# A two-layer attention and MLP block, forward and backward, in one kernel: weights read in fewer passes, half of one product on VectorE, PSUM rearranged for it

## The chip, the cores and the metric

The kernel runs on one core of a Trainium2 chip. The metric is the device time of one execution, in microseconds (us), smaller being better. The kernel before the change takes 559.78 us (median of three runs, 557.5 to 561.76). Each execution is classed as fast or slow by its time against the fastest run of the same kernel. The span in a profile is 1.5 us shorter than the time of the same execution (560.3 beside 561.76 for the kernel before).

In the text, PE is TensorE (matmuls), DVE is VectorE, ACT is ScalarE, POOL is GpSimd and SP is SyncE. PE, DVE and ACT do arithmetic here; SP issues loads and the writes of zeros, POOL issues the stores of results.

## The reference, cut to what matters

There is one token, D = 1024, 32 query heads in 4 groups, a window of the last 4096 of 32768 cached keys, F = 3584, all in bf16. The same two layers are applied twice with the same weights, and the kernel returns the output and the gradients of eight inputs.

```python
def _fwd_reference(A_x, A_k_cache, A_v_cache, A_wq, A_wo, B_x, B_w1, B_b1, B_w2):
    # _A_ref: attention over the window, q = x @ wq, result @ wo
    def _B_ref(x, w1, b1, w2):
        h = x @ w1 + b1
        act = h * tanh(softplus(h))                 # Mish
        return act @ w2
    x = A_x
    x = x + _A_ref(_layernorm(x), A_k_cache, A_v_cache, A_wq, A_wo)   # layer 1, "A1"
    x = x + _B_ref(_layernorm(x), B_w1, B_b1, B_w2)                   # layer 2, "B2"
    x = x + _A_ref(_layernorm(x), ...)                                # layer 3, "A3"
    x = x + _B_ref(_layernorm(x), ...)                                # layer 4, "B4"
    return x

_out, _vjp = jax.vjp(_f, A_x, A_k_cache, A_v_cache, A_wq, A_wo, B_w1, B_b1, B_w2)
return (_out, *_vjp(grad_out))
```

(The lines are shortened.) Three consequences matter. All products have one column, so a weight that passes through PE is used once per pass: forward as it lies, backward after a transpose on PE (eight 128x128 transposes into PSUM, then a copy back by ACT or DVE). The gradients of w1, w2, wq, wo, and of K and V inside the window, are sums of two outer products, which must be written out in full: 78 parts of 448 or 512 KB. And the gradients of the caches outside the window are zeros, 112 writes of 512 KB that depend on nothing and can be placed anywhere.

## The kernel before: the parts that matter

Everything runs in program order on each engine. The PSUM pools of the first part add up to 16 KB per partition: four transpose tiles of 2 KB ("pt"), one of 4 KB ("pbig"), two accumulators of 2 KB ("pacc").

```python
pt = tc.alloc_tile_pool(name="pt", bufs=4, space=PSUM)       # 4 x 2 KB
pbig = tc.alloc_tile_pool(name="pbig", bufs=1, space=PSUM)   # 4 KB
pacc = tc.alloc_tile_pool(name="pacc", bufs=1, space=PSUM)   # acc and sm, 2 KB each
...
def zeros(n):                                    # n zero writes on the SP queue
    for _ in range(min(n, len(zero_jobs))):
        nc.sync.dma_start(zero_jobs.pop(0), zt[:])

def xpose2(halves):                              # 2 x 8 transposes, then two copies
    pss = []
    for blocks, dst in halves:
        ps = psum1([P, 8, P], BF16, "tps")
        for b, ap in enumerate(blocks):
            nc.tensor.transpose(ps[:, b, :], ap, ident_bf[:])
        pss.append(ps)
    for (blocks, dst), ps in zip(halves, pss):
        evac(dst, ps...)                         # DVE or ACT, whichever has less to do
...
# order of the work: w1 is read 4 times, w2 3 times
x1, sA1 = attn_fwd(x0, "A1", True)
x2, sB2 = mlp_fwd(x1, "B2", None)        # w1, w2
x3, sA3 = attn_fwd(x2, "A3", False)
x4, sB4 = mlp_fwd(x3, "B4", gcolb)       # w1, then w2 forward and w2 * grad_out
g3, g3b = mlp_bwd_w1(gcol, "B4", sB4, "A3")   # w1
g2, g2b = attn_bwd(g3, g3b, "A3", sA3, True, "B2")
mlp_bwd_w2(g2b, "B2", sB2)               # w2
g1, g1b = mlp_bwd_w1(g2, "B2", sB2, "A1")     # w1
g0, g0b = attn_bwd(g1, g1b, "A1", sA1, False, "X0")
zeros(1000)                              # all zero writes not yet issued
```

When the last gradient of x is there, the three PSUM pools are released and replaced by four output tiles of 4 KB. An output part is made by four matmuls into two tiles, a cast of each tile to bf16 (one on DVE, one on ACT, as a rule), and one store on the POOL queue:

```python
pacc.release(); pbig.release(); pt.release()
pools["p2"] = tc.tile_pool(name="p2", bufs=4, space=PSUM)    # 4 x 4 KB
...
for c in range(nblk // 2):
    st = stage_tile([P, 2, D], "st_t")
    pss = [psum2([P, 1024], FP32, "ops") for _ in range(2)]
    for i in range(2):
        for tt in range(2):
            b = 2 * c + tt
            outer(R, b % 4, (b // 4) * P, i * 512, pss[tt][:, i * 512:(i + 1) * 512])
    for tt in range(2):
        ev_out(st[:, tt, :], pss[tt][:])         # cast PSUM -> SBUF
    nc.gpsimd.dma_start(out_v[c], st[:])
```

Of the kernel before, what the change touches and what calls it, by code (L numbers as in the profile page):

```python
# [14 lines left out]
P = 128  # L15
# [3 lines left out]
NB = 5  # L19
NR = 8  # L20
# [3 lines left out]
def kernel(  # L24
# [47 lines left out]
    pt = tc.alloc_tile_pool(name="pt", bufs=4, space=bass.MemoryType.PSUM)  # L72
    pbig = tc.alloc_tile_pool(name="pbig", bufs=1, space=bass.MemoryType.PSUM)
    pacc = tc.alloc_tile_pool(name="pacc", bufs=1, space=bass.MemoryType.PSUM)
# [21 lines left out]
    rows0 = work.tile([P, 512], BF16, name="rows0", tag="e32", padded_shape=[P, 2 * WC])  # L96
# [36 lines left out]
    def evac(out_ap, in_ap, cd, ca):  # L133
        if ev[0] + cd <= ev[1] + ca:
            ev[0] += cd
            nc.vector.tensor_copy(out_ap, in_ap)  # L136
        else:
            ev[1] += ca
            nc.scalar.copy(out_ap, in_ap)  # L139
# [12 lines left out]
    def psum1(shape, dtype, name):  # L152
        if "p2" in pools:
            return psum2(shape, dtype, name)
        return shaped(pt.tile([P, 512 if dtype == FP32 else 1024], dtype, name=name, tag="pt"), shape)

    def psum2(shape, dtype, name):
        if "p2" in pools:
            return shaped(pools["p2"].tile([P, 1024 if dtype == FP32 else 2048], dtype, name=name, tag="p2"), shape)
        return shaped(pbig.tile([P, 1024 if dtype == FP32 else 2048], dtype, name=name, tag="big"), shape)  # L160

    def xpose2(halves):

        pss = []
        for blocks, dst in halves:
            ps = psum1([P, 8, P], BF16, "tps")
            for b, ap in enumerate(blocks):
                nc.tensor.transpose(ps[:, b, :], ap, ident_bf[:])  # L168
            pss.append(ps)
        for (blocks, dst), ps in zip(halves, pss):  # L170
            n = len(blocks)
            evac(dst, ps[:, 0:n, :].rearrange("p b c -> p (b c)"), 0.08 * n + 0.03, 0.11 * n + 0.15)
# [18 lines left out]
    xq = []  # L191

    def fill(n):
        for _ in range(min(n, len(xq))):
            xpose2([nat_blocks(ap) for ap in xq.pop(0)])
# [98 lines left out]
    def row_layout(col32, name):  # L294
        x = work.tile([P, G, DH], BF16, name=name, tag="rx", bufs=2)
        ps = psum1([P, P], BF16, "rps")
        nc.tensor.transpose(ps[:, 0:P], col32[:], ident_bf[:])
        for g in range(G):
            nc.vector.tensor_scalar(out=x[:, g, :], in0=ps[:, 0:P], scalar1=gmask[:, g:g + 1], scalar2=None, op0=ALU.mult)  # L299
        return x  # L300
# [29 lines left out]
    def to_kpart(src, name):  # L330
        ps = psum1([P, TJ, P], BF16, "kps")
        for j in range(TJ):
            nc.tensor.transpose(ps[:, j, :], src[:, j * P:(j + 1) * P], ident_bf[:])
        dst = work.tile([P, TJ, P], BF16, name="kpart", tag="e32", padded_shape=[P, 2 * TJ, P])
        h = TJ // 2
        nc.vector.tensor_copy(dst[:, 0:h, :], ps[:, 0:h, :])
        nc.scalar.copy(dst[:, h:, :], ps[:, h:TJ, :])
        return dst

    def attn_fwd(x_col, lname, first):  # L340
        n32, n_bf, rstd = ln_fwd(x_col, lname)
        sv = dict(n32=n32, rstd=rstd)
        pad = pad_tile("q_pad")
        acc = acc_tile(HQ)
        wo_ld = {}
        if first:
            for t in range(TD):
# [4 lines left out]
            load_kv(keep, K_t, k_v, "K")  # L352
            load_kv(vpool, V_t, v_v, "V")
            for c in range(NR):
                wo_load(c)
        for t in range(TD):
            for h in range(HQ):
                mm(acc[:, h:h + 1], wq_t[2 * t + h // 16][:, (h % 16) * P:(h % 16 + 1) * P], n_bf[:, t:t + 1],
                   t == 0 and h == 0, t == TD - 1)
        sv["qrep"] = pad_cols(pad, acc[:], scale, f"q_{lname}")  # L360
        if first:
            for g in range(G):
                for u in range(2):
                    xpose2([nat_blocks(flat(K_t[g])[:, (2 * u + k) * 1024:(2 * u + k + 1) * 1024]) for k in range(2)])
        else:
            for w in wq_t:
                xq.append([w[:, k * 1024:(k + 1) * 1024] for k in range(2)])
        big = psum2([P, WC], FP32, "big")
        rows_mm(big, pad, K_t)
        if not first:  # L370
            for g in range(G):
                for u in range(2):
                    xq.append([flat(K_t[g])[:, (2 * u + k) * 1024:(2 * u + k + 1) * 1024] for k in range(2)])
# [4 lines left out]
        m32 = work.tile([1, NC, 32], FP32, name="m32")  # L378
# [5 lines left out]
        e32 = work.tile([P, WC], FP32, name="e32", tag="e32")  # L384
        ssum = work.tile([P, 1], FP32, name="ssum")
        nc.scalar.activation(e32[:], big[:], ACT.Exp, bias=nm[:, 0:1], scale=1.0, accum_out=ssum[:, 0:1])
# [5 lines left out]
        nc.vector.tensor_scalar(out=p_bf[:], in0=e32[:], scalar1=rs[:, 0:1], scalar2=None, op0=ALU.mult)  # L392
# [4 lines left out]
        if not first:  # L397
            for g in range(G):
                for u in range(2):
                    xq.append([flat(V_t[g])[:, (2 * u + k) * 1024:(2 * u + k + 1) * 1024] for k in range(2)])  # L400
# [5 lines left out]
        o_row = work.tile([HQ, P], BF16, name="o_row")  # L406
# [9 lines left out]
        for i, c in enumerate(order):  # L416
            w = wo_kept[c] if c < NR else wo_load(c)
            if i == NB - 1:
                zeros(Z["A1" if first else "A3"])
            fwd_rows2(yacc, w, c, o_bf, i == 0, i == NO - 1)  # L420
        x_new = keep.tile([P, TD], FP32, name=f"x_{lname}")
        nc.vector.tensor_add(x_new[:], x_col[:], yacc[:])
        return x_new, sv

    def mlp_fwd(x_col, lname, g_bf):
# [4 lines left out]
        for i in range(2 * TD):  # L430
            t, hf = i // 2, i % 2
            w = w1_load(i)
            if i == NB - 1:
                zeros(Z[lname])
# [4 lines left out]
            if g_bf is not None:  # L439
                zeros(1 if i >= 2 else 0)  # L440
                fill(2)
        h = work.tile([P, TF], FP32, name="h")
        nc.vector.tensor_add(h[:], hacc[:], b1_f[:])
        hm = work.tile([P, TF], FP32, name="hm")
        nc.vector.tensor_scalar(out=hm[:], in0=h[:], scalar1=20.0, scalar2=None, op0=ALU.min)
        u = work.tile([P, TF], FP32, name="u")
        nc.scalar.activation(u[:], hm[:], ACT.Exp)
        w_ = work.tile([P, TF], FP32, name="w_")
        nc.vector.scalar_tensor_tensor(out=w_[:], in0=u[:], scalar=2.0, in1=u[:], op0=ALU.add, op1=ALU.mult)
        r = work.tile([P, TF], FP32, name="r")  # L450
        nc.vector.tensor_scalar(out=r[:], in0=w_[:], scalar1=2.0, scalar2=None, op0=ALU.add)
        nc.vector.reciprocal(r[:], r[:])
        t_f = work.tile([P, TF], FP32, name="t_f")
        nc.vector.tensor_mul(t_f[:], w_[:], r[:])
        a_bf = pair_col("a", lname, TF)
        nc.vector.tensor_mul(a_bf, h[:], t_f[:])

        v1 = work.tile([P, TF], FP32, name="v1")
        nc.vector.scalar_tensor_tensor(out=v1[:], in0=t_f[:], scalar=1.0, in1=r[:], op0=ALU.add, op1=ALU.mult)
        v2 = work.tile([P, TF], FP32, name="v2")  # L460
        nc.vector.tensor_scalar(out=v2[:], in0=u[:], scalar1=1.0, scalar2=None, op0=ALU.add)
        nc.vector.reciprocal(v2[:], v2[:])
        nc.vector.tensor_mul(v2[:], v2[:], u[:])
        nc.vector.tensor_mul(v1[:], v1[:], v2[:])
        nc.vector.tensor_mul(v1[:], v1[:], h[:])
        dact = keep.tile([P, TF], FP32, name=f"dact_{lname}")
        nc.vector.scalar_tensor_tensor(out=dact[:], in0=v1[:], scalar=2.0, in1=t_f[:], op0=ALU.mult, op1=ALU.add)
        sv["dact"] = dact
        acc = acc_tile(TD + TF)
        yacc, dacc = acc[:, 0:TD], acc[:, TD:]  # L470
        held = []
        for c in range(NW2):
            w = w2_load(c)
            fwd_rows2(yacc, w, c, a_bf, c == 0, c == NW2 - 1)
            if g_bf is not None:
                if c >= 2:
                    zeros(c % 2)
                xpose_rows2(w)
                if held:
                    bwd_rows2(dacc, held.pop(), c - 1, g_bf)  # L480
                held.append(w)
        if g_bf is not None:
            bwd_rows2(dacc, held.pop(), NW2 - 1, g_bf)
            dh_of(dacc, lname, sv)
        x_new = keep.tile([P, TD], FP32, name=f"x_{lname}")
        nc.vector.tensor_add(x_new[:], x_col[:], yacc)
        return x_new, sv

    def dh_of(dacc, lname, sv):
        dh = keep.tile([P, TF], FP32, name=f"dh_{lname}")  # L490
        nc.vector.tensor_mul(dh[:], dacc, sv["dact"][:])
# [3 lines left out]

    def mlp_bwd_w2(g_bf, lname, sv):
        dacc = acc_tile(TF)
        ws = {}

        def T(c):  # L500
            ws[c] = w2_load(c)
            if c == NB - 1:
                zeros(Z["bw2"])
            xpose_rows2(ws[c])

        pipe(list(range(NW2)), T, lambda c, i: bwd_rows2(dacc, ws.pop(c), c, g_bf, started=i > 0))
        dh_of(dacc[:], lname, sv)

    def mlp_bwd_w1(g_col, lname, sv, nxt):
# [3 lines left out]
        def T(i):  # L513
            w = w1_load(i)
            ws[i] = w
            zeros(1 if i % 8 == 7 else 0)
# [11 lines left out]
    def attn_bwd(g_col, g_bf, lname, sv, first, nxt):  # L528
        dacc = acc_tile(HQ)
        pad = pad_tile("do_pad")  # L530
        ws = {}
        loaded = {}

        def T(c):
            if c + NR < NO:
# [283 lines left out]
```

## Time and profile before

| stage of the kernel before | ends at, us | length, us |
|---|---|---|
| layer 1 forward | 78.4 | 78.4 |
| layer 2 forward | 117.5 | 39.1 |
| layer 3 forward | 158.6 | 41.1 |
| layer 4 forward and its input gradient | 265.2 | 106.6 |
| layer 3 backward | 319.8 | 54.6 |
| layer 2: w2 backward | 344.0 | 24.2 |
| layer 2: w1 backward | 374.6 | 30.6 |
| layer 1 backward | 426.9 | 52.3 |
| outputs | 560.3 | 133.4 |

The stage ends were read from the timeline. Three lines of the page of the profile of the kernel before give the span, the clock of PE over 40 slices of it (in tenths of full speed, so a 5 is half) and the bytes:

```profile
span 560.3 us, 15939 instructions
...
PEclk9996555555569996677976599767755555555555
...
HBM read 89.14 MB, written 98.58 MB: 335 GB/s over the span
```

The windows view gives, for a stretch from A to B (us), its length, each engine's busy time, then the granted PE clock, the busy share of the 16 DMA engines and the rate. These are stretches of the kernel before: layer 2 forward, layer 4, w2 backward, and the outputs.

```profile
core 0: us, PE busy (x) PEld busy (x) DVE busy (x) ACT busy (x) POOL busy (x), PEclk, DMA share, GB/s
...
78.40:117.50 39.10, 16.53 (x450) 14.43 (x450) 4.00 (x22) 0.72 (x3) 0.00 (x0) 0.50 0.94 359
...
158.60:265.20 106.60, 91.38 (x1870) 89.98 (x1871) 54.55 (x105) 48.70 (x53) 0.00 (x0) 0.82 0.90 324
...
319.80:344.00 24.20, 20.27 (x450) 19.49 (x448) 12.00 (x20) 11.01 (x11) 0.00 (x0) 0.96 0.80 264
...
426.90:560.30 133.40, 93.74 (x559) 36.22 (x559) 93.04 (x118) 86.48 (x86) 45.65 (x80) 0.50 0.83 313
```

The limits change. Layer 2 forward waits for DMA (share 0.94; PE is busy 16.5 of 39.1 us). In layer 4 PE is busy 91.4 of 106.6 us. In the outputs no single busy time fills the stretch; the timeline of the kernel before (start, length, engine, line, operation, count merged into one line, and in brackets the idle time before it and what ended it) shows the reason:

```profile
431.07 4.72 DVE L136 CAST st_t<-ops 128x1024 bf16<-128x1024 f32 x4
...
434.03 0.53 POOL L644 DMA_DIRECT2D out_dram<-st_t  x1 [0.63 <-ACT st_t L139]
...
434.17 3.06 ACT L139 CAST st_t<-ops 128x1024 bf16<-128x1024 f32 x3 [0.18 <-PE ops L188]
...
435.16 0.53 POOL L644 DMA_DIRECT2D out_dram<-st_t  x1 [0.60 <-DVE st_t L136]
...
436.35 0.53 POOL L644 DMA_DIRECT2D out_dram<-st_t  x1 [0.65 <-ACT st_t L139]
```

Four DVE casts follow each other without a gap (4.72 us, 1.18 us each), and the stores leave about 1.16 us apart. While the steady stores run, the casts are the limit. The first store is at 431.7 us.

### The profile page before, as it was taken

The numbers are of one execution on the slowest core, as the hardware profiler recorded it, in microseconds if no ns is written. First come the engines' busy times: TensorE is split into PE (matmuls) and PEld (weight loads), VectorE is DVE, ScalarE is ACT, GpSimd is POOL, SyncE is SP. The second block draws the span as 40 slices with busy tenths as digits, with TensorE's granted clock in tenths as the row PEclk, the third lists the DMA queues.
The fourth block names the chain that finished last, engine by engine and source line by source line (L and its number), as shares of the span: only waits on it lengthen the run. The fifth ranks groups of instructions, "written<-read, shape, count | busy, mean of one in ns | idle before, by whom it ended". The sixth has DMA issues, their size and how long they took to land. (4 is left out here: it accounts for less than half of the span.)

```text
span 560.3 us, 15939 instructions
## 1 busy us (share of the span) xinstructions
PE 384.5 (69%) x7058; PEld 305.6 (55%) x7058; DVE 228.9 (41%) x411; ACT 192.4 (34%) x211; POOL 51.0 (9%) x95
## 2 busy tenths in 40 slices
PE   3384254364589979877966688768675756888790
PEld 3373153362589979867954677768362112146510
DVE  2052000102037753334632155324304866977691
ACT  1041000001027733333530144323102786855591
POOL 2000000000000000000000000000001423433341
PEclk9996555555569996677976599767755555555555
DMA  8999989999799979789599888896998978797986
GB/s 306 416 418 408 414 301 381 400 400 416 265 384 388 409 243 321 259 282 322 205 363 405 351 277 295 273 349 216 418 414 361 383 308 323 305 341 255 301 349 251
DMA packets 51041, 188.76 MB, mean 337 GB/s; under 512 B 5888, under 2 KB 5916, under 8 KB 49948
## 3 DMA queue, kind: packets, MB, share of 16 engines
q1 hardware_dynamic: 40624, 147.87, 69.9%
q0 software_dynamic: 10304, 39.86, 19.0%
q8 instruction: 55, 0.90, 0.6%
q14 instruction: 14, 0.11, 0.1%
q10 hardware_dynamic: 44, 0.01, 0.0%
HBM read 89.14 MB, written 98.58 MB: 335 GB/s over the span
## 5 line engine op out<-in xcount | busy, mean ns | idle before, releaser
L168 PE MATMUL tps<-ident_bf,w_c 128*128 128x128 bf16 x896 | 72.9, 246 | 16.3 <-DMA w_c<-in_B_w_dram 16.0
L188 PEld LDWEIGHTS <-w_c 128*128 128x128 bf16 x1792 | 57.8, 100 | 33.8 <-DMA w_c<-in_B_w_dram 23.8
L139 ACT COPY w_c<-tps 128x1024 bf16<-128x1024 bf16 (+1 forms) x50 | 46.2, 927 | 84.4 <-PE tps L168 79.5
L168 PEld LDWEIGHTS <-w_c 128*128 128x128 bf16 x896 | 62.8, 112 | 17.9 <-DMA w_c<-in_B_w_dram 17.9
L136 DVE COPY w_c<-tps 128x1024 bf16<-128x1024 bf16 (+1 forms) x70 | 46.0, 667 | 64.6 <-PE tps L168 60.8
L139 ACT CAST st_t<-ops 128x1024 bf16<-128x1024 f32 x32 | 31.3, 1014 | 23.4 <-PE ops L188 21.6
L136 DVE CAST st_t<-ops 128x1024 bf16<-128x1024 f32 x28 | 33.0, 1220 | 6.9 <-issue 3.3
L188 PEld LDWEIGHTS <-wo_c 128*128 128x128 bf16 x512 | 16.4, 102 | 22.6 <-DMA wo_c<-in_A_wo_dram 21.8
L188 PE MATMUL acc<-a_pair,w_c 128*128 128x1 bf16 x448 | 15.8, 165 | 17.2 <-DMA w_c<-in_B_w_dram 12.3
L209 ACT ACTIVATE lnv<-var,eps_t 128x1 f32<-128x1 f32 x4 | 1.2, 294 | 72.5 <-DVE var L206 72.5
L168 PE MATMUL tps<-ident_bf,wo_c 128*128 128x128 bf16 x256 | 21.2, 249 | 5.6 <-DMA wo_c<-in_A_wo_dram 5.6
L188 PE MATMUL acc<-nB_pair,w_c 128*128 128x1 bf16 x448 | 15.8, 165 | 12.4 <-DMA w_c<-in_B_w_dram 9.3
L589 POOL DMA_DIRECT2D out_dram<-rt x2 | 1.2, 594 | 251.3 <-DVE rt L588 224.4
L188 PE MATMUL acc<-o_pair,wo_c 128*128 128x1 bf16 x256 | 8.7, 166 | 21.2 <-DMA wo_c<-in_A_wo_dram 20.9
L136 DVE COPY wo_c<-tps 128x1024 bf16<-128x1024 bf16 x20 | 13.7, 691 | 21.2 <-PE tps L168 20.6
L136 DVE CAST st_kv<-ops 128x1024 bf16<-128x1024 f32 x15 | 18.3, 1225 | 9.8 <-PE ops L188 7.0
L139 ACT CAST st_kv<-ops 128x1024 bf16<-128x1024 f32 x17 | 17.0, 1014 | 14.4 <-PE ops L188 14.4
L168 PEld LDWEIGHTS <-wo_c 128*128 128x128 bf16 x256 | 18.3, 113 | 6.0 <-DMA wo_c<-in_A_wo_dram 6.0
L139 ACT COPY wo_c<-tps 128x1024 bf16<-128x1024 bf16 x12 | 12.1, 1012 | 22.3 <-PE tps L168 21.1
L188 PE MATMUL ops<-Ro 2*128 2x512 bf16 x64 | 16.8, 602 | 3.1 <-ACT st_t L139 1.9
L644 POOL DMA_DIRECT2D out_dram<-st_t x30 | 16.0, 534 | 26.5 <-DVE st_t L136 18.1
L136 DVE CAST st_wq<-ops 128x1024 bf16<-128x1024 f32 x15 | 17.2, 1217 | 1.8 <-ACT st_wq L139 0.8
(501 smaller groups left out, 708.2 us busy)
## 6 DMA issues: line engine op xcount, KB each, us to landing
out_dram<-zt SPq DMA_DIRECT2D x112, 512.0 KB, 8.7
w_c<-in_B_w_dram SPq DMA_DIRECT2D x64, 448.0 KB, 5.6
w_c<-in_B_w_dram SPq DMA_DIRECT2D x42, 512.0 KB, 5.9
wo_c<-in_A_wo_dram SPq DMA_DIRECT2D x32, 512.0 KB, 7.6
out_dram<-st_t POOLq DMA_DIRECT2D x30, 512.0 KB, 4.9
out_dram<-st_kv POOLq DMA_DIRECT2D x16, 512.0 KB, 5.2
out_dram<-st_wq POOLq DMA_DIRECT2D x16, 512.0 KB, 5.1
K_180<-in_A_k_cache_dram SPq DMA_DIRECT2D x1, 1024.0 KB
```

Source lines behind the costliest of these rows:

```text
L136: nc.vector.tensor_copy(out_ap, in_ap)
L139: nc.scalar.copy(out_ap, in_ap)
L168: nc.tensor.transpose(ps[:, b, :], ap, ident_bf[:])
L188: nc.tensor.matmul(out_ap, lhsT=lhsT, rhs=rhs, start=start, stop=stop, skip_group_check=True, **kw)
L209: nc.scalar.activation(lnv[:], var[:], ACT.Ln, bias=eps_t[:, 0:1], scale=1.0)
L589: nc.gpsimd.dma_start(out_flat.rearrange("(n p) -> n p", p=P), rt[0:n, :])
L644: nc.gpsimd.dma_start(out_v[c], st[:])
```

## The change

Its intent is to read w1 three times instead of four and w2 twice instead of three. The gradient that enters layer 4's w2 is grad_out itself, known from the start. So the first pass over w2 (layer 2 forward) can also compute w2 * grad_out. Then layer 4 needs w2 only for its output, which nothing waits for, and this is put into the pass over w2 that layer 2's backward needs anyway. With w2 * grad_out known, one block of 512 columns of w1 is enough to go forward, through Mish, and backward at once; layer 4 becomes seven such blocks. To relieve PE in the two w2 passes, one of each pair of w2 rows is multiplied by the gradient and summed on DVE instead of being transposed and multiplied on PE; that needs the gradient copied to all partitions (a broadcast).

PSUM is rearranged for it: transposes use two tiles of 4 KB, and the three pools stay to the end, so that the outputs have these two tiles and "pbig", three in all. One more stream buffer and one more kept part of wo are paid for with one output staging buffer less. The zero writes are placed anew.

The core of the diff, with cuts:

```diff
-    pt = tc.alloc_tile_pool(name="pt", bufs=4, space=PSUM)        # 2 KB each
+    pt = ctx.enter_context(tc.tile_pool(name="pt", bufs=2, ...))  # 4 KB each
...
+    turn = [0]
+    def psum_out(shape, dtype, name):
+        turn[0] += 1
+        return (psum2 if turn[0] % 3 == 0 else psum1)(shape, dtype, name)
...
+    def w2_pass(a_bf, g_bf, x_col, xname, wgname, zk):
+        gbc = bcast_row(g_bf)
+        ...
+        for c in range(NW2):
+            w = w2_load(c)
+            fwd_rows2(yacc, w, c, a_bf, c == 0, c == NW2 - 1)
+            ps = psum1([P, 8, P], BF16, "tps")
+            for b in range(TD):
+                nc.tensor.transpose(ps[:, b, :], w[:, 1, b * P:(b + 1) * P], ident_bf[:])
+            nc.scalar.copy(w[:, 1, :], ps[:].rearrange("p b c -> p (b c)"))
+            nc.vector.tensor_tensor_reduce(out=scr[:], in0=w[:, 0, :], in1=gbc[:], ...,
+                                           op0=ALU.mult, op1=ALU.add, accum_out=wg[:, c, 0:1])
+            if held:
+                bwd1(held.pop(), c - 1)
+            held.append(w)
...
+    def mlp_turn(x_col, lname, wg, g_col, nxt):
+        def T(b):
+            zeros(Z["B4"])
+            ws[b] = [w1_block(b, hh) for hh in range(2)]       # two loads, [128, 4, 512]
+            ... 32 forward matmuls into hps ...
+            for hh in range(2):
+                wf = ws[b][hh][:].rearrange("p t f -> p (t f)")
+                xpose2([alt_blocks(...) for k in range(2)], "a" if hh == 0 else None)
+                if hh == 0:
+                    mish(hps[:], lo, FB, a_bf[:, lo:lo + FB], da)
+                    nc.vector.tensor_mul(dh[:, lo:lo + FB], da, wgf[:, lo:lo + FB])
+                    nc.vector.tensor_copy(dh_bf[:, lo:lo + FB], dh[:, lo:lo + FB])
+            fill(2, ["V", "K", "wo", "wq"])                    # transposes for later
+        def M(b, _): ... 32 backward matmuls with dh_bf ...
+        pipe(list(range(NBK)), T, M)
...
-            pss = [psum2([P, 1024], FP32, "ops") for _ in range(2)]
+            pss = [psum_out([P, 1024], FP32, "ops") for _ in range(2)]
...
-    Z = dict(A1=6, B2=1, A3=18, B4=1, bw2=19)
+    Z = dict(A3a=10, A3b=6, B4=2, B4end=3, A3c=4, A3d=16, A1c=4, A1d=16)
...
     x1, sA1 = attn_fwd(x0, "A1", True)
-    x2, sB2 = mlp_fwd(x1, "B2", None)
+    x2, sB2, wg4 = mlp_fwd(x1, "B2", gcolb)
     x3, sA3 = attn_fwd(x2, "A3", False)
-    x4, sB4 = mlp_fwd(x3, "B4", gcolb)
-    g3, g3b = mlp_bwd_w1(gcol, "B4", sB4, "A3")
+    g3, g3b, sB4 = mlp_turn(x3, "B4", wg4, gcol, "A3")
     g2, g2b = attn_bwd(g3, g3b, "A3", sA3, True, "B2")
-    mlp_bwd_w2(g2b, "B2", sB2)
+    x4, wg2 = w2_pass(sB4["a_bf"], g2b, x3, "x_B4", "wg2", 5)
...
-    pacc.release()
-    pbig.release()
-    pt.release()
-    pools["p2"] = ctx.enter_context(tc.tile_pool(name="p2", bufs=4, space=PSUM))
```

## The prediction

> **What bounds it now.** Stretches, by the windows view and the timeline. To 158 us (layers 1 to 3 forward) the DMA queue mostly binds: 0.88 to 1.02 of DMA busy, 326 to 413 GB/s. From 198 to 386 us (layer 4 and most of the backward) TensorE and stream buffers bind: PE busy 80 to 90%, DMA only 263 to 350 GB/s; sixteen transposes cost 0.9 us (warm clock) or 1.7 (cold). From 431 us to the end outputs bind on PSUM evacuation: one 512 KB store per 1.13 us, DVE casts of 1.22 and ACT casts of 1.02 us in parallel, clock 0.50.
>
> **What the change does.**
> 1. Reads fall from 89.1 to 72.9 MB (w1 and w2 7.3 MB less each, wo 1.6 MB). At 413 GB/s (windows, 28 to 57 us) that is 39 us of DMA time. The gain is rather the removed stages: layer 4's w2 (199 to 232 us) and separate w1 backward (232 to 263 us).
> 2. It adds: a DVE multiply-reduce per w2 chunk in both passes (1.22 us in the trace; a load takes 1.26); a grad broadcast of about 2 us per pass; layer 4 as 7 column blocks. In a block a serial chain runs: 32 forward matmuls 0.8, 16 transposes 0.9, two ACT copies 2.0, exp 0.3, eleven tiny DVE operations 2.1, DVE copy 0.7, transposes 0.9, backward matmuls 0.8. With only two transpose tiles I estimate 8.8 us per block, 62 us in all, against 5.2 us of pure PE work.
> 3. It moves 13 wq transpose units (about 14 us) onto layer 3's attention backward, which gains as much by not transposing kept wo.
> 4. It takes output PSUM from four 4 KB tiles to three. PSUM has 8 banks per partition (the Trainium skill, "Trainium Kernel Development and Optimization", NeuronCore Architecture); all stay allocated. In the trace a freed tile needs 1.09 us to the next cast, then 1.02 or 1.22 us of cast. Each pair's second tile must now wait for the preceding pair; PE issues in order, so the pair period becomes about 0.05+0.75+1.1 = 1.9 us instead of 1.13. For 62 pairs that is +47 us; for the 16 K/V pairs, 1.7 to about 3, +18 us.
>
> **On the critical path (before, after, estimate).** x1 78, 70; x2 117, 112; x3 158, 160; layer 4's input gradient 265, 232; layer 3's 320, 287; layer 2's 374, 335; first output store 431, 390. Head: about -41 us; output phase: 129 to about 190 us. Pure sum 580 us. I lean below that because fills and zero writes look tuned: 568 us, range 533 to 597. Faster 0.27, same 0.27, slower 0.46.
>
> **What would show it.** DMA page: reads near 73 MB. Tile view of the layer-4 blocks: about 8 to 9 us each. Output stores about 1.9 us apart, with PE waiting on ACT or DVE casts where before casts were back to back; TensorE clock still 0.5 there. Before, it was 0.50 from 57 to 158 us, PE 40 to 60% busy. The skill's "TensorE: Matmul & The Clock Gate" (Part 1) says an idle window of about 3.4 us throttles it to half; the idle gaps inside blocks might do that and cost more.
>
> **What would make it wrong.** Blocks running near 5.2 us (total about 550); three output tiles overlapping better, at best 3 tiles per 2.3 us, which is 1.5 us per pair (25 us less); the 1 KB column-block rows loading slowly.

## The result, and the profile after

The kernel after takes 590.29 us (median of 586.75, 588.65, 591.93 and 593.9), the kernel before on the same chip 558.64 us (four runs). The ratio is 1.0567, with a 95% interval of 1.0504 to 1.063: it is slower by 5.7%. Here and below, the ratio is from fast runs alone, so it need not be quite the ratio of the medians that are quoted. The profile is of the run of 586.75 us, the fastest; of the others there is none.

The same three lines of the page of the kernel after:

```profile
span 584.8 us, 14928 instructions
...
PEclk9965555557967968677855887655555555555555
...
HBM read 72.89 MB, written 98.58 MB: 293 GB/s over the span
```

The reads did fall, by 16.25 MB, and so did the number of instructions. The windows view of the kernel after, for layer 2 forward, layer 4, the w2 pass, the first part of the outputs, and all of the outputs (columns as there):

```profile
70.40:116.00 45.60, 30.70 (x682) 29.16 (x682) 21.20 (x49) 14.89 (x17) 0.00 (x0) 0.50 0.86 311
...
162.50:236.10 73.60, 52.74 (x948) 50.43 (x949) 33.38 (x129) 35.00 (x44) 0.00 (x0) 0.78 0.61 201
...
295.20:321.00 25.80, 22.56 (x456) 21.90 (x456) 18.78 (x37) 14.17 (x14) 0.00 (x0) 0.50 0.71 256
...
394.10:459.40 65.30, 30.21 (x143) 6.99 (x144) 36.31 (x47) 34.98 (x33) 16.70 (x32) 0.50 1.02 398
...
394.10:584.80 190.70, 96.34 (x559) 35.61 (x559) 97.11 (x118) 88.23 (x86) 45.65 (x80) 0.50 0.73 281
```

| stage | before, us | after, us | difference |
|---|---|---|---|
| layer 1 forward | 78.4 | 70.4 | -8.0 |
| layer 2 forward, now with w2 * grad_out | 39.1 | 45.6 | +6.5 |
| layer 3 forward | 41.1 | 46.5 | +5.4 |
| layer 4 and its input gradient | 106.6 | 73.6 | -33.0 |
| layer 3 backward | 54.6 | 59.1 | +4.5 |
| w2 pass (layer 4's output, layer 2's w2 backward) | 24.2 | 25.8 | +1.6 |
| layer 2: w1 backward | 30.6 | 27.3 | -3.3 |
| layer 1 backward | 52.3 | 45.8 | -6.5 |
| outputs | 133.4 | 190.7 | +57.3 |
| sum | 560.3 | 584.8 | +24.5 |

So the part that the change is about was won: everything up to the outputs is 32.8 us shorter, and layer 4 is 33.0 us shorter. The outputs, whose arithmetic is the same (559 matmuls before and after, and DVE, ACT and POOL busy within 4.1 us of before), take 57.3 us more. The timeline of the kernel after shows what became of the gapless casts:

```profile
405.17 1.14 PE L188 MATMUL ops<-R 2*128 2x512 bf16 x4 [0.62 <-ACT st_t L139]
...
405.82 1.01 ACT L139 CAST st_t<-ops 128x1024 bf16<-128x1024 f32 x1 [0.70 <-PE ops L188]
...
406.21 1.23 DVE L136 CAST st_t<-ops 128x1024 bf16<-128x1024 f32 x1 [0.54 <-PE ops L188]
...
406.88 1.19 PE L188 MATMUL ops<-R 2*128 2x512 bf16 x4 [0.57 <-ACT st_t L139]
...
407.58 1.01 ACT L139 CAST st_t<-ops 128x1024 bf16<-128x1024 f32 x1 [0.75 <-PE ops L188]
...
407.93 1.22 DVE L136 CAST st_t<-ops 128x1024 bf16<-128x1024 f32 x1 [0.48 <-PE ops L188]
```

ACT's cast ends at 406.83 us; PE's next four matmuls start at 406.88; ACT's next cast starts at 407.58 and frees its tile at 408.59. PE waits for a cast, and both casts wait for PE, in turn. The reason is visible in the allocation: with three tiles, a pair of tiles always shares one tile with the pair before it, so its second tile is free only when a cast of that pair is done. With four tiles, the pair before owns the other two. The Trainium skill ("Perfetto Trace Analysis", Optimization Strategy) says that a gap which repeats on the engine that should be saturated can mean that there is too little SBUF or PSUM for the next tile. This trace agrees: gaps of 0.48 to 0.75 us before every cast.

The waits view of the output stretch sums this up (engine, what it waited for, us in total, times, longest). First the kernel before, then the kernel after:

```profile
PE ops L188 <- ACT st_t L139: 3.7, 8, 1.1
```

```profile
PE ops L188 <- ACT st_t L139: 14.1, 20, 1.2
...
PE ops L188 <- ACT st_w L139: 12.9, 11, 1.4
...
PE ops L188 <- ACT st_wq L139: 11.3, 12, 1.2
```

The kernel before has smaller waits of the same kind that these lines do not show (the view lists its casts of w1 one tile at a time). Added up over all casts of the outputs, PE waited 11.1 us in 25 waits before and 70.3 us in 74 waits after: 59.2 us more, about the 57.3 us that were lost.

There is a second thing in the window 394.1 to 459.4 above: DMA is saturated there (share 1.02, 398 GB/s). In the kernel after, 19 zero writes are issued after the first store, the last at 437.4 us, and they move until 463.8 us; in the kernel before there is none. The DMA view of 420 to 470 us lists the transfers (count, size, median us from issue to landing), first before, then after:

```profile
out_dram<-zt SPq DMA_DIRECT2D x4, 512.0 KB, 10.4
...
out_dram<-st_w_8172 POOLq DMA_DIRECT2D x1, 448.0 KB, 4.7
```

```profile
out_dram<-st_w POOLq DMA_DIRECT2D x16, 448.0 KB, 13.2
out_dram<-zt SPq DMA_DIRECT2D x7, 512.0 KB, 24.3
```

Before the change, the slowest of these stores of w1's gradient landed 4.7 us after its issue; after the change, the median is 13.2 us. The Trainium skill ("DMA: Bandwidth & Descriptors", Queues, rings and completion order) says that each DMA engine takes turns between the queues that have work, packet by packet. The trace agrees, as the DMA view of 430 to 440 us shows (queue, packets, MB, share; q0 carries the stores, q1 the zero writes):

```profile
q0 software_dynamic: 536, 2.03, 52.1%
q1 hardware_dynamic: 536, 1.95, 50.2%
```

From 440 to 450 us it is 426 packets beside 428, though 2.41 MB beside 1.56 MB: the packets are shared equally, and those of w1's stores are larger.

So two causes compete for the longer outputs: three tiles, or zero writes that were left over by a shorter head.

### The profile page after: what moved, and what is told of

Read it like the earlier page. It is cut to its first block, busy times and chain, and to the rows that moved or that the text cites. A ratio compares the mean times of both kernels' runs of the same rounds, so it can differ in the third digit from the quotient of the medians.

```text
span 584.8 us, 14928 instructions
## 1 busy us (share of the span) xinstructions
PE 382.0 (65%) x6610; PEld 297.6 (51%) x6610; DVE 247.0 (42%) x495; ACT 209.2 (36%) x231; POOL 51.0 (9%) x95
## 3 DMA queue, kind: packets, MB, share of 16 engines
HBM read 72.89 MB, written 98.58 MB: 293 GB/s over the span
## 5 line engine op out<-in xcount | busy, mean ns | idle before, releaser
L188 PEld LDWEIGHTS <-w_c 128*128 128x128 bf16 x1120 | 39.0, 105 | 17.5 <-DMA w_c<-in_B_w_dram 10.1
L188 PE MATMUL ops<-R 2*128 2x512 bf16 x120 | 27.2, 569 | 30.3 <-ACT st_w L139 12.9
L188 PEld LDWEIGHTS <-wq 128*128 128x128 bf16 x1024 | 29.3, 104 | 18.7 <-DMA wq<-in_A_wq_dram 13.1
L484 ACT COPY w_c<-tps 128x1024 bf16<-128x1024 bf16 x28 | 28.3, 1012 | 28.7 <-PE tps L483 22.1
L486 DVE CUSTOM_DVE_ANT_0 scr<-w_c,gbc 128x1024 bf16<-128x1024 bf16 x28 | 34.2, 1221 | 9.3 <-DMA w_c<-in_B_w_dram 6.5
L136 DVE CAST st_kv<-ops 128x1024 bf16<-128x1024 f32 x15 | 18.4, 1225 | 27.7 <-PE ops L188 24.5
L169 PE MATMUL tps<-ident_bf,K 128*128 128x128 bf16 x256 | 23.4, 265 | 9.7 <-ACT w_b L139 6.2
L139 ACT COPY w_b<-tps 128x1024 bf16<-128x1024 bf16 x23 | 22.4, 1016 | 17.9 <-PE tps L169 15.2
L483 PE MATMUL tps<-ident_bf,w_c 128*128 128x128 bf16 x224 | 28.4, 308 | 0.0
L136 DVE COPY K<-tps 128x1024 bf16<-128x1024 bf16 x20 | 13.4, 687 | 30.6 <-PE tps L169 22.4
L169 PEld LDWEIGHTS <-K 128*128 128x128 bf16 x256 | 20.8, 122 | 10.7 <-issue 10.7
L139 ACT CAST st_w<-ops 128x768 bf16<-128x768 f32 (+1 forms) x17 | 18.9, 1125 | 12.7 <-PE ops L188 12.7
L136 DVE CAST st_wq<-ops 128x1024 bf16<-128x1024 f32 x15 | 18.4, 1225 | 11.0 <-PE ops L188 11.0
```

The costliest lines, as they stand in the source:

```text
L136: nc.vector.tensor_copy(out_ap, in_ap)
L139: nc.scalar.copy(out_ap, in_ap)
L169: nc.tensor.transpose(ps[:, i, b, :], ap, ident_bf[:])
L188: nc.tensor.matmul(out_ap, lhsT=lhsT, rhs=rhs, start=start, stop=stop, skip_group_check=True, **kw)
L483: nc.tensor.transpose(ps[:, b, :], w[:, 1, b * P:(b + 1) * P], ident_bf[:])
L484: nc.scalar.copy(w[:, 1, :], ps[:].rearrange("p b c -> p (b c)"))
```

## The experiments

Theory T: the number of output tiles sets the outputs' time; zero writes bind only behind it. Rival Z: the zero writes do it, since they hold the DMA engines while the stores need them. Theory B: layer 4's blocks are held by the hand-overs between PE, ACT and DVE, and not by the w1 loads or by PE's work. All kernels below gave correct results. The kernel before ran in the same rounds: 561.64 us for the first four experiments, 557.2 us for the next four, 559.53 us for the last (medians). "Against after" is worked out as the difference of the two ratios to before, times 560 us.

### 1. Four output tiles again

```diff
 # kernel after
+    pacc.release()
+    pbig.release()
+    pt.release()
+    pools["p2"] = ctx.enter_context(tc.tile_pool(name="p2", bufs=4, space=PSUM))
     dw_tall(rows["w2"], ...)           # psum1 and psum2 now take from p2
```

> The changed kernel, only that the three PSUM pools are released before the outputs and four 4 KB output tiles are taken, as in the kernel before. Theory T (three output tiles): the output stretch falls from 190.7 us back to 133 to 143 us, store pairs about 1.13 us apart, so 528 to 540 us in all, below both kernels. Rival R1 (the zero writes still under way when the outputs begin, to about 437 us, take the DMA engines from the output stores): those writes stay, the stretch stays above 170 us and the total above 565 us.

Measured: 552.43 us median; ratio 0.9757 (0.967 to 0.9845), which is about 45 us less than after. Two of its four runs count as slow only because one run was exceptionally quick (544.54 beside 552.08, 552.77 and 553.17); so the ratio rests on two runs, its verdict at 2% is unclear, and the direction is not. The outputs took 149.0 us in the profile, 41.7 less than after. The gain is real and by far the largest single one, but it missed the expected 528 to 540 us. Where the rest stayed is in the windows and on POOL's timeline of this kernel:

```profile
401.10:463.40 62.30, 30.76 (x151) 8.10 (x152) 36.38 (x49) 34.45 (x33) 16.72 (x32) 0.50 1.02 398
```

```profile
437.19 0.54 POOL L853 DMA_DIRECT2D out_dram<-st_w  x1 [2.16 <-DMA out_dram<-st_t]
439.86 0.54 POOL L853 DMA_DIRECT2D out_dram<-st_w  x1 [2.12 <-DMA out_dram<-st_t]
```

The first 62 us, up to the 30th store (the last of w1's), are DMA-bound at the very same share and rate as in the kernel after, 1.02 and 398 GB/s, and stores wait for earlier stores to land. The w1 stores leave 2.26 us apart, the wo stores behind them 1.19 us apart. So theory T was incomplete: with the tiles out of the way, the zero writes bind in the first half.

### 2. Three output tiles in the kernel before

```diff
 # kernel before
-    pools["p2"] = ctx.enter_context(tc.tile_pool(name="p2", bufs=4, space=PSUM))
+    pools["p2"] = ctx.enter_context(tc.tile_pool(name="p2", bufs=3, space=PSUM))
```

> The kernel before, only with three output tiles in place of four (one number). Theory T: the output stretch grows from 133 to about 190 us, about 615 us in all. Rival R1 (zero writes over the outputs): the zero writes of this kernel are done as the outputs begin, so the time stays within 555 to 568 us.

Measured: 616.21 us, ratio 1.0968 (1.0931 to 1.1004). The code up to the outputs is unchanged, and the outputs took 189.7 us, against 190.7 in the kernel after; the spacing of stores was 1.96, 1.93, 1.94, 2.80 and 1.76 us for w2, w1, wo, K/V and wq, against 1.87, 1.99, 1.91, 2.85 and 1.82 after. The windows line of this kernel's outputs:

```profile
423.90:613.60 189.70, 97.75 (x559) 35.19 (x559) 96.22 (x117) 89.08 (x86) 45.66 (x80) 0.50 0.57 219
```

DMA is at 0.57 only. One number in the kernel before reproduces the whole loss, and no zero write is left over here. For the kernel after this settles that three tiles suffice as a cause; it does not say that the zero writes would be harmless without them, as experiment 1 shows.

### 3. Zero writes earlier, three tiles kept

```diff
         def T(b):
-            zeros(Z["B4"])
             ws[b] = [w1_block(b, hh) for hh in range(2)]
+            zeros(Z["B4"])
...
-    Z = dict(..., B4=2, ..., A3d=16, ...)
+    Z = dict(..., B4=4, ..., A3d=28, ...)
```

> The changed kernel, with 26 of its 112 zero writes moved from the end of the queue to the layer-4 blocks (4 a block, after the block's loads) and to layer 3's attention backward, so that hardly any are left when the outputs begin. Theory T: the output stretch stays within 5 us of 190 us and the total between 578 and 592 us. Rival R1: the output stretch falls by 15 to 40 us, with the total between 545 and 570 us.

Measured: 594.56 us, ratio 1.058 (1.0547 to 1.0614): no change against after. The total is a little above the expected band; in its profile the head was 7.5 us longer than in the profile of the kernel after (401.6 beside 394.1 us), while the outputs took the same 190.7 us. No zero write is issued after the first store. The windows line of the first part of the outputs:

```profile
401.60:466.80 65.20, 30.15 (x142) 6.94 (x143) 36.26 (x46) 34.99 (x33) 16.66 (x31) 0.50 0.57 227
```

The same number of results takes 65.2 us instead of 65.3, with DMA at 0.57 instead of 1.02. A saturated DMA was relieved of almost half its work, and nothing got faster. Rival Z falls as the sole cause.

### 4. Three tiles, but one tile's matmuls together

```diff
-            for i in range(2):
-                for tt in range(2):
+            for tt in range(2):
+                for i in range(2):
...
-            for q in (0, 2, 1, 3):
+            for q in (0, 1, 2, 3):
```

> The changed kernel, with three output tiles, but the matmuls of a pair issued tile by tile (both halves of the first tile, then both of the second) instead of alternating; the K and V gradients are left as they are. It tests the second half of theory T, that a free tile's second matmul sits behind the wait of the other tile: then 62 pairs go from about 1.8 to 1.9 us to about 1.5 us and the total falls by 18 to 25 us to 562 to 572 us. If only the number of tiles counted and the order did not (T without the order), or if R1 held, the time stays within 5 us of the changed kernel's.

Measured: 574.27 us, ratio 1.0212 (1.0176 to 1.0249), about 20 us less than after; just outside the expected band. The outputs took 174.1 us. The order of matmuls is then part of the mechanism: in the kernel after the four matmuls alternate between the two tiles, so PE, which works in order, holds back the free tile's second matmul behind the first one for the tile that is not yet free. With the order changed, wo's stores come 1.57 us apart instead of 1.91 and wq's 1.28 instead of 1.82; K/V, which was left as it was, stays at 2.85. The w1 stores do not gain (2.15); they lie where the zero writes bind.

### 5. Four tiles and zero writes earlier

This is 1 and 3 together.

> The changed kernel with four output tiles and 26 zero writes moved forward, both at once (each alone was run: 552 and 595 us). Theory T+R1 (with three tiles the wait on casts hides the zero writes still under way; with four tiles those writes become the limit): the output stretch falls to 131 to 138 us, the total to 528 to 541 us. If the zero writes are not what held the four-tile run at 149 us of output, it stays at 550 to 560 us.

Measured: 536.41 us, ratio 0.9623 (0.9566 to 0.9681), within what was expected: 53 us less than after and 3.8% less than before. The outputs took 133.1 us, as in the kernel before (133.4), and the store spacing is that of before (1.17, 1.18, 1.19, 1.69, 1.13). The first part of its outputs in the windows view, up to the 30th store, and four DVE casts from its timeline, again without a gap:

```profile
403.30:447.70 44.40, 30.21 (x143) 7.38 (x144) 34.55 (x46) 33.36 (x33) 16.75 (x32) 0.50 0.81 312
```

```profile
410.81 4.68 DVE L136 CAST st_t<-ops 128x1024 bf16<-128x1024 f32 x4
```

The four kernels make a square for the first part of the outputs: both limits 65.3 us, tiles alone 65.2, zero writes alone 62.3, neither 44.4. (The stretches end as the 30th store is issued; POOL's count, 31 or 32, has two small stores more, and in experiment 3 the 30th falls just behind the end.) Each limit hides almost wholly behind the other: with the other still there, removing the zero writes gains 0.1 us and removing the three-tile limit 3.0 us; removing both gains 20.9 us. A single experiment would have understated one of them.

This run also settles the smaller staging pool of the changed kernel, which it keeps: with one output staging buffer less the outputs take no longer than before.

### 6. A third transpose tile in layer 4's blocks

"pbig" is idle while the blocks run. Here every third transpose takes it.

```diff
-        ps = psum1([P, 2, 8, P], BF16, "tps")
+        if turn_on[0]:                       # true only around pipe(...) of mlp_turn
+            turn_on[1] += 1
+            ps = (psum2 if turn_on[1] % 3 == 0 else psum1)([P, 2, 8, P], BF16, "tps")
+        else:
+            ps = psum1([P, 2, 8, P], BF16, "tps")
```

> The changed kernel, with three transpose tiles in place of two in layer 4's column blocks (the third is the 4 KB tile that is idle there). Theory B (a block of 8.4 us is a chain of waits for free tiles: TensorE waits for two ACT copies and then for VectorE's tiny operations): blocks fall to 6.3 to 7.4 us, layer 4's stretch by 8 to 14 us, the total by as much. Rival R2 (the blocks are slow because TensorE runs at half clock in parts of them, or because the column-block reads are slow): less than 4 us.

For comparison, one block in the timeline of the kernel after:

```profile
192.74 0.94 PE L188 MATMUL sm<-nB_pair,w_b 128*128 128x1 bf16 x32
193.53 1.95 PE L169 MATMUL tps<-ident_bf,w_b 128*128 128x128 bf16 x32
194.62 1.93 ACT L139 COPY w_b<-tps 128x1024 bf16<-128x1024 bf16 x2 [1.48 <-PE tps L169]
196.44 0.22 ACT L444 ACTIVATE u<-hm 128x4 f32<-128x4 f32 x1
196.60 1.05 PE L169 MATMUL tps<-ident_bf,K 128*128 128x128 bf16 x16 [1.12 <-ACT w_b L139]
196.69 0.16 DVE L445 SCALAR_TENSOR_TENSOR w__3464<-u 128x4 f32<-128x4 f32 x1 [2.55 <-ACT u L444]
...
198.63 0.69 DVE L136 COPY w_b<-tps 128x1024 bf16<-128x1024 bf16 x1
199.38 1.05 PE L169 MATMUL tps<-ident_bf,K 128*128 128x128 bf16 x16 [1.72 <-DVE w_b L136]
200.27 0.94 PE L188 MATMUL acc<-dh_pair,w_b 128*128 128x1 bf16 x32
```

PE stands twice, 1.12 us for ACT's copies and 1.72 us for DVE's copy, because both transpose tiles are full. Between the two, ACT's exp stands in line behind its own two copies, and DVE's copy behind Mish's small operations.

Measured: 576.47 us, ratio 1.034 (1.0271 to 1.0408), about 13 us less than after. A block takes 6.47 us instead of 8.95, and layer 4's stretch in the windows view shrinks to this:

```profile
165.70:221.00 55.30, 44.10 (x948) 42.12 (x948) 32.49 (x130) 34.14 (x44) 0.00 (x0) 0.93 0.70 236
```

The stretch gave 18.3 us, more than expected; the total gave less than the stretch. PE's busy time fell by 8.6 us (52.74 to 44.10) and the time in which it was not busy by 9.7 us. The clock rose from 0.78 to 0.93, so the first part is likely to be faster transposes and matmuls after fewer gaps; that was not tested apart. Theory B holds: neither the loads nor the amount of PE work changed.

### 7. Mish before the first transposes

```diff
             for hh in range(2):
-                xpose2([...], "a" if hh == 0 else None)
+                if hh == 1:
+                    xpose2([...], None)
                 if hh == 0:
                     mish(hps[:], lo, FB, a_bf[:, lo:lo + FB], da)
                     ...
+                    xpose2([...], "a")
```

> The changed kernel, with the block's activation chain written before the first transposes' two ACT copies, so that its exp on ACT no longer stands behind 2 us of copies. Theory B: the chain is 2 us shorter a block, 6.4 to 7.2 us a block, 9 to 14 us less in all. Rival R2: less than 4 us.

Measured: 580.62 us, ratio 1.042 (1.0357 to 1.0483), about 8 us less than after. A block takes 7.67 us, so the size of the gain per block was expected too large (6.4 to 7.2 us). The stretch:

```profile
165.30:230.10 64.80, 49.16 (x948) 46.82 (x949) 34.10 (x130) 35.67 (x44) 0.00 (x0) 0.84 0.67 223
```

The exp behind the copies is one part of the chain, and the missing tile the larger part. The two gains do not add, as experiment 9 shows.

### 8. All of w2's backward on PE

```diff
-            (8 transposes, ACT copy, tensor_tensor_reduce on VectorE)
+            xpose_rows2(w)                    # 16 transposes, two copies
...
-                bwd1(held.pop(), c - 1)
+                bwd_rows2(dacc, held.pop(), c - 1, g_bf)
```

> The changed kernel with one part undone: all of w2's backward is transposed and multiplied on TensorE again, nothing on VectorE, and no grad broadcast. In the changed kernel a w2 pass takes about 1.49 us a chunk at clock 0.50 plus 3 us of broadcast, about 25 us. If the VectorE half is worth something, each pass grows: at the warm clock to about 1.7 to 1.9 us a chunk (1 to 3 us a pass after the broadcast is saved, 2 to 6 us in all), at the half clock to about 2.9 us a chunk (17 us a pass, 35 us in all). If it is worth nothing, the total stays within 3 us.

Measured: 605.61 us, ratio 1.081 (1.0708 to 1.0912), about 14 us more than after. Layer 2 forward ends at 124.2 us instead of 116.0, and the second pass takes 29.1 us instead of 25.1 (from layer 3's gradient to the output of the pass). The VectorE half is therefore worth its broadcast. The size matches neither of the two that were expected, 2 to 6 us at the warm clock and 35 us at the half clock: the granted clock was 0.75 in the first pass (90 to 123.8 us) and 0.82 in the second. The clock makes it a less simple comparison: within the second pass, first of the kernel after, then of this one:

```profile
297.00:320.00 23.00, 21.60 (x446) 21.03 (x444) 17.20 (x28) 14.17 (x14) 0.00 (x0) 0.50 0.76 273
```

```profile
311.00:339.50 28.50, 27.36 (x648) 26.87 (x646) 11.46 (x17) 11.13 (x11) 0.00 (x0) 0.82 0.70 232
```

With the VectorE half, PE is busy 94% of the pass and stays at half clock throughout; with all work on PE the clock warms to 0.82 and the pass is still longer, having twice the transposes per chunk on PE. The Trainium skill ("TensorE: Matmul & The Clock Gate", Part 1) says that the clock goes to full speed after one window of about 3.4 us of sustained activity. The pass of 23.0 us in which PE was busy for 21.6 us does not agree with this reading of "busy"; what the clock counts as activity was not settled by these runs.

### 9. All that helped, together

Four output tiles, three transpose tiles in the blocks, Mish first, zero writes behind the block loads (B4=3, A3d=28).

> The changed kernel with all of it together: four output tiles, three transpose tiles in the column blocks, exp ahead of the copies, 3 zero writes a block (after its loads) and 28 in layer 3's attention backward. From the four-tile run with early zeros (536 us): three transpose tiles alone took 15 to 20 us from layer 4's stretch and the exp alone 10 us; together the blocks should reach about 5.5 to 6 us, near TensorE's own 5.2 us, so 511 to 521 us in all, an 8% gain over the kernel before. If the blocks are then held by the DMA queue (2 loads and 3 zero writes a block are 6.3 us), 518 to 526 us.

Measured: 517.86 us median of six runs, ratio 0.9293 (0.9232 to 0.9353). This is 7.1% below the kernel before and about 71 us below the kernel after; it beats both. Layer 4's gradient ends at 219.7 us, layer 1's at 382.7 us, and the outputs take 133.2 us (span 515.9). Layer 4's stretch:

```profile
163.10:219.70 56.60, 47.55 (x948) 46.38 (x948) 33.91 (x130) 35.22 (x44) 0.00 (x0) 0.86 0.84 303
```

The total fell where it was expected, but the blocks did not: 6.52 us each (165.56 to 204.66 us, six blocks), where 5.5 to 6 us were forecast. The third tile alone gave 6.47 us, so Mish first added nothing to it here. In these blocks (166 to 212 us) PE waits 2.3 us for w1 loads, against 0.2 us in experiment 6 (168 to 214 us), and DMA is at 0.84 instead of 0.70; three zero writes a block instead of two may be the reason, which was not tested.

So the plan of fewer passes was sound, and what it lost lay in what was rearranged along with it.

## Why the prediction was wrong

It said 568 us, and 590.29 us were measured; it had the chances at 0.27 for faster, 0.27 for the same and 0.46 for slower. The mechanism was right and the size was off. Taken point by point:

- **Three output tiles.** Right. The prediction put the outputs at about 190 us from the first store and the pair at 1.9 us; measured are 186.2 us (398.6 to 584.8) and 1.82 to 1.99 us, K/V 2.85 with "about 3" forecast. Experiments 1, 2 and 5 show it as the cause. The expected +61 us was +57.6. That the total of this term came out was in part luck: the zero writes left over at the first store are not in it, and by themselves they hold the first part of the outputs at 62.3 us (experiment 1) against 65.3; only because the two limits do not add did the omission cost nothing.
- **Layer 4's blocks.** Right. 8.8 us per block were estimated, 8.95 measured (six blocks in 53.71 us); the layer took 73.6 us against 72. Experiments 6 and 7 show that the hand-overs hold it.
- **The reads.** Right: 72.89 MB, and the gain came from removed stages, not from the bytes. DMA's share in layer 4 fell from 0.90 to 0.61.
- **The head.** Forecast -41 us to the first store, measured -33.1. Layer 2 forward ended at 116.0 us, not 112: its w2 pass ran at clock 0.50 and needed 1.49 us per chunk, where one load's 1.26 us had been assumed: 3.2 us more over 14 chunks. The broadcast was not it: it took 1.6 us (91.54 to 93.11 us), where about 2 us had been assumed. Layer 3 backward took 59.1 us, not 55: the wq transposes, all on the chain, took 18.4 us, not 14. Layer 2 backward took 53.1 us, not 48. The last stage to the first store was 4.7 us shorter than forecast.
- **The step that failed.** "I lean below that because fills and zero writes look tuned: 568 us." The sum of the terms was 580 us, and 12 us were taken off with nothing in the profile to stand for them. The span came out at 584.8 us: nothing of the 12 us was there to be had, and the sum itself was short by 4.8 us. The zero writes were not tuned for the shorter head: 19 of them were left over at the first store. Experiment 3 shows that placing them better gains nothing while three tiles bind, and experiment 5 that they cost nearly as much as three tiles do in the first part once the tiles are there (62.3 against 44.4 us; three tiles 65.2). The lean had no term behind it that could pay.

The sum works out: 12 us for the lean, 8 us for the head, 3.4 us back from the outputs, 2 us between the span and the time of a run, and 3.5 us between the profiled run and the median, together 22.1 of the 22.3 us that were missing. The last two are not effects of the change. The measured time lies within the range of 533 to 597 us.

What stays open: heads of the same code differed by about 7 us between profiles (394.1 us in the profile of the kernel after, 401.1 and 401.0 us in experiments 1 and 4, which changed nothing there; 401.6 and 403.3 us in experiments 3 and 5, which moved zero writes within the head). The difference is spread over the stages; the largest part of it between the kernel after and experiment 1, 2.7 us, lies in layer 3 forward (46.5 and 49.2 us, at clock 0.72 and 0.67). Its cause stays open, and differences of a few us in the head are therefore not read as effects here. The clock's half speed in the w2 pass is unexplained as well.

## What to carry to other kernels

A change that rearranges PSUM or SBUF for one stage must be costed in every stage that inherits the arrangement: here one output tile fewer turned gapless casts into a ping-pong and cost more than all the saved passes brought. Where two limits stand behind each other, removing one shows little or nothing; remove both before calling either harmless. And when the terms of a forecast have been added up, keep the sum, unless a line of the profile pays for the discount.

## What the Trainium skill lacked or had wrong

- "TensorE: Matmul & The Clock Gate" (Part 1) leaves open what counts as activity. In the w2 pass PE was busy 21.60 of 23.00 us, weight loads 21.03, and the clock was 0.50 throughout; with twice the transposes per chunk (experiment 8) it was 0.82 at a busy time of 27.36 of 28.50 us. In the outputs it was 0.50 in every kernel, with PE busy 93.74 of 133.40 us in the kernel before.
- "PSUM — Partial Sum Buffer" gives no cost for handing a tile back and forth between PE and the casts. Here a pair of fp32 tiles of up to 128x1024 took 1.13 to 1.19 us with four tiles (casts back to back), 1.82 to 1.99 us with three (kernel after; both without the K/V pairs), and 1.28 to 1.57 us with three and one tile's matmuls together where zero writes did not bind.
- "Perfetto Trace Analysis" (Optimization Strategy) has the repeating gap, which fitted, but not that a second limit can hide behind it: 65.3 us with both, 65.2 and 62.3 us with one removed, 44.4 us with both removed.
- "DMA: Bandwidth & Descriptors" (Queues, rings and completion order) has the turn-taking of queues, which fitted (536 against 536 packets in 10 us); no page says what it means for a store that competes with bulk writes: 448 KB landed after 13.2 us (median), and after 2.8 us in experiment 3, with the same three tiles and no zero writes left.
